# Blocks of 256 tokens: the activation's high half made by GpSimd, and one weight conversion moved from before the first block into it

## The chip, the cores and the metric

The kernel runs on one core of a Trainium2 chip. The metric is the device time of one execution in microseconds (us). A core has a matrix engine (TensorE, PE in the rows; its weight loads are PEld), a vector engine (VectorE, DVE), a scalar engine (ScalarE, ACT), a general engine (GpSimd, POOL) and a queue that only issues transfers here (SyncE, SP). Each engine takes its own instructions in a fixed order and waits on semaphores for the others.

## The reference, cut to what matters

Windowed causal attention feeds two MLPs in a row; everything is float32, the weights arrive as float64.

```python
# 4 batches, 8 heads, 576 positions, head size 64, window of 128 keys
scores = scale * q @ k.T ;  scores = where(mask, scores - slope*|i-j|, -1e9)
attn = exp(scores - max) ;  attn = attn / (attn.sum() + 1e-9)
x = attn @ v                                  # -> [2304 tokens, 512]
h = x @ w_in1                                 # [2304, 2048]
g = where(h >= 1, h, where(h <= -1, 0, (h + 1)**2 / 4))
x = g @ w_out1                                # [2304, 512]
h = x @ w_in2 ;  g = h * clip(h + 3, 0, 6) / 6
out = g @ w_out2
```

## The kernel before, in words

TensorE multiplies in a rounded float32 type, so every operand exists as two parts: a high half (the value rounded to that type) and a low half (the value less its high half). A product is the sum of three matmuls: low by high, high by low, high by high. The function `split_hi` (lines 150 to 156) makes a high half on a named engine: on ACT a copy (line 152), on "pool" a GpSimd multiplication by 1.0 (line 154). `split_lo` (lines 158 and 159) subtracts on a named engine.

The attention works in units of 64 to 256 query positions; unit 0 has 256 positions, two steps for each of the 8 heads, 16 steps in all. One `att.tick()` does one step's scores (stage a: matmuls at line 411, DVE bias and row minimum at 441, ACT exponential at 445) and the later stages of earlier steps (transposes at 469 and 470, copies at 152, product with the values at 506 or 554). For a pair of heads it then normalizes (518 to 520), transposes (531) and splits the result into x (152 and 159), one 128-row chunk of x for each pair. Units 0 to 3 go this way; later units use a longer one with more GpSimd work (389 to 403, 450, 488).

The first MLP takes tokens in blocks: three of 256 (0, 1 and 2), then four of 384. For every one of 16 chunks f of the hidden layer, `first` computes h (line 659, 12 matmuls), `activate` computes g (688 on DVE, 689 on ACT, 690 on DVE, high half at 691 on ACT, low half at 692 on GpSimd), and two chunks later `second` multiplies g with w_out (line 701, 12 matmuls). Blocks 0 and 1 are each done in two halves of 8 chunks, in the order 0A, 1A, 0Z, 1Z, since weights are still arriving; block 2 and the wide blocks take all 16 chunks.

The weights of chunk f (1 MB of float64) are loaded and converted in place. `conv_tick` (222 to 233) finishes chunk n-1 (`conv2`: DVE lines 205 and 212; `conv3`: ACT high half at 152, DVE low half at 159, the tile `wa`) and begins chunk n (`conv1`: ACT at 194 and 198, GpSimd at 197). A chunk f can be used once the tick numbered f+2 is through. Before the first block there are `n_pre` = 20 ticks of attention, t = 0 to 19 (lines 862 to 868); conversions are traced after t = 9, 14, 18 and 19. Inside half-blocks the function `spread` (870 to 883) calls conversion and attention ticks from a hook that runs twice per chunk, 16 times per half-block: after slot k, `ceil(conv * k / 16)` conversions are done.

SyncE issues its transfers in the order of the program. On the other engines a planner puts the instructions in order from modelled times: among those that it thinks ready, the one earliest in the program goes first, so a later one can fill a gap. Some instructions are tied behind others (`att.behind()`).

Of the kernel before, what the change touches and what calls it, by code (L numbers as in the profile page):

```python
# [29 lines left out]
HI = dict(v="act", th="act", xf="act", x="act", g="act", x2="act")  # L30
# [10 lines left out]
def tile_window_attention_two_mlps(  # L41
# [20 lines left out]
    KF = DFF // P  # L62
# [11 lines left out]
    N1, WIDE = 256, 384  # L74
# [75 lines left out]
    def split_hi(eng, hi, x):  # L150
        if eng == "act":
            nc.scalar.copy(hi, x)  # L152
        elif eng == "pool":
            nc.gpsimd.tensor_scalar(out=hi, in0=x, scalar1=1.0, scalar2=1.0, op0=ALU.mult, op1=ALU.mult)
        else:
            engines[eng].tensor_copy(hi, x)

    def split_lo(eng, lo, x, hi):
        engines[eng].tensor_tensor(out=lo, in0=x, in1=hi.bitcast(F32), op=ALU.subtract)  # L159
# [105 lines left out]
    unit_steps = [sum(1 for n, _ in steps if heads[n].unit == j) for j in range(len(units))]  # L265
# [406 lines left out]
    class Mlp1(Mlp):  # L672
# [11 lines left out]
        def activate(self, ps, n):  # L684


            r, g = self.tiles()
            nc.vector.tensor_scalar(out=r[:, :n], in0=ps[:, :n], scalar1=-1.0, scalar2=1.0, op0=ALU.max, op1=ALU.min)  # L688
            self.square = nc.scalar.activation(out=r[:, :n], in_=r[:, :n], func=AF.Square, bias=0.5, scale=0.5)  # L689
            self.larger = nc.vector.tensor_tensor(out=r[:, :n], in0=ps[:, :n], in1=r[:, :n], op=ALU.max)  # L690
            split_hi(HI["g"], g[:, 0, :n], r[:, :n])
            split_lo(LO[self.g_lo], g[:, 1, :n], r[:, :n], g[:, 0, :n])
            return g

# [139 lines left out]
    A, Z = range(KF // 2), range(KF // 2, KF)  # L834

    def run_block(mlp1, j, part, hook):
        for f in part:
            chunks.run(mlp1, j, f, part, j, lambda: hook(f, 0), lambda: hook(f, 1), att.behind)

    with ExitStack() as actx:  # L840
        mlp1 = Mlp1(W1, blocks1, rpool, gpool)
# [20 lines left out]
        n_pre = unit_steps[0] + LAG_D  # L862
        for t in range(n_pre):
            att.tick()
            if t % 2 == 0:
                W1.load()
            if t in (n_pre // 2 - 1, n_pre - 6) or t >= n_pre - 2:
                W1.conv_tick()

        def spread(part, ticks, conv):  # L870

            slots = 2 * len(part)
            att0, conv0 = att.t, W1.n_conv

            def hook(f, after):
                k = 2 * (f - part[0]) + after + 1
                W1.load()
                while W1.n_conv < conv0 + min(conv, -(-conv * k // slots)) and W1.conv_tick():
                    pass
                while att.t < att0 + min(ticks, -(-ticks * k // (slots - 2))):  # L880
                    att.tick()

            return hook
# [14 lines left out]

            return hook

        run_block(mlp1, 0, A, spread(A, unit_steps[1] + unit_steps[2], KF // 2 - 2))
        run_block(mlp1, 1, A, spread(A, 10, KF // 4))
        att.make_tables()
        run_block(mlp1, 0, Z, spread(Z, unit_steps[3] - 10, KF // 2))
# [259 lines left out]
    for m, blk, f, part, g in chunks.pend:  # L1164
        assert f == KF - 1
        t0, n = m.blocks[blk]
# [138 lines left out]
    for j, x in enumerate((xa, xb)):  # L1305
        block = Block(j, x)
        for i in range(KF // 2):
            def hook(n):
                if j == 0 and n == 0:
                    if 1 <= i <= 5:  # L1310
                        weight_sums(i + 2)
                    if i in (4, 6):
                        xb.load((i - 4) // 2)
                    if i in (6, 7):
                        xb.make(i - 6, lambda: ts.tile([P, N2], F32, tag="t", name="t"))
                spare((0.5, 0.8, 0, 0.8, 0, 0, 0.4)[n])
                load_operands()
# [30 lines left out]
```

## Time and profile before

| | |
|---|---|
| time, median of 3 runs (lowest to highest) | 946.75 us (946.28 to 947.42) |
| the profiled execution's own time | 946.02 us |
| span of its trace | 944.3 us |
| busy share of the span: PE, PEld, DVE, ACT, POOL | 98%, 93%, 70%, 57%, 32% |
| granted TensorE clock, mean | 1.000 |
| chain that ended last: PE, DVE, ACT, DMA, POOL | 89%, 5%, 2%, 2%, 1% |

Busy shares are means over stages that differ much, so the windows are read stage by stage. A matmul counts as busy from its issue to the end that the profile models, so a busy PE can still issue fewer matmuls than it could. The first matmuls of `first` run at about 23 us, the first instruction at line 688 starts at 36.17 us, half-block 0A lasts to about 75 us and the three blocks of 256 tokens to about 230 us. After 500 us there is no GpSimd work left.

### The profile page before, as it was taken

What the parts mean: (1) busy time and instruction counts of PE and PEld (TensorE: products, weight loads), DVE (VectorE), ACT (ScalarE), POOL (GpSimd) and SP (SyncE); (2) the same over time, 40 slices, a digit from 0 to 9 for tenths busy, and PEclk for the clock granted to TensorE, in tenths of its full rate; (3) what the DMA queues carried; (4) which work ended last, traced back from release to release, by engine and by line L of the source; (5) the groups of instructions that cost most, each with busy time, mean ns of one, the idle gap of its engine ahead of it and who ended that gap; (6) DMA issues with size and microseconds to landing.
All of it is one profiled execution on the core that took longest, in us unless ns stands there. A gap on an engine that the chain in (4) does not pass through costs nothing.

```text
span 944.3 us, 17237 instructions
## 1 busy us (share of the span) xinstructions
PE 928.5 (98%) x5683; PEld 875.5 (93%) x5683; DVE 659.4 (70%) x1750; ACT 535.6 (57%) x1349; POOL 306.8 (32%) x575
## 2 busy tenths in 40 slices
PE   8899999999999999999999999999999999999998
PEld 6799999999999999999999999999999888898987
DVE  6998975786677677767656899958557777644443
ACT  6998854676667566666635786535333334423233
POOL 3243845787668676777710000000000000000000
PEclk9999999999999999999999999999999999999999
DMA  8858322232222212322017771004264654543431
GB/s 256 240 178 264 111 89 88 68 86 67 73 64 72 79 46 62 89 75 62 1 55 270 266 237 55 1 23 167 81 210 170 232 174 146 169 124 114 123 112 67
DMA packets 95337, 114.90 MB, mean 122 GB/s; under 512 B 8848, under 2 KB 73616, under 8 KB 95248
## 3 DMA queue, kind: packets, MB, share of 16 engines
q1 hardware_dynamic: 95248, 113.80, 38.3%
q8 instruction: 45, 0.74, 0.3%
q14 instruction: 44, 0.36, 0.1%
HBM read 88.60 MB, written 25.17 MB: 120 GB/s over the span
## 4 chain that ended last, share of the span: by engine, by line
PE 89%; DVE 5%; ACT 2%; DMA 2%; issue 1%; POOL 1%; SPq 0%; ACTq 0%; DVEq 0%; POOLq 0%
PE h L659 26%; PE acc L760 21%; PE acc L701 18%; PE y L1249 7%; PE x L1249 5%; PE s L411 4%; PE r L554 3%; PE t L470 2%; PE r L506 2%; DMA rawa<-w_in 1%; DVE r L688 1%; DVE kl L391 1%; DVE r L690 1%; DVE x L159 1%; DMA kw<-kT 1%
## 5 line engine op out<-in xcount | busy, mean ns | idle before, releaser
L659 PE MATMUL h<-x,wa 128*128 128x384 f32 (+1 forms) x1344 | 231.0, 317 | 1.4 <-DVE r L690 0.9
L701 PE MATMUL acc<-g,wa 128*128 128x384 f32 (+1 forms) x1344 | 227.4, 315 | 0.4 <-POOL g L159 0.4
L760 PE MATMUL acc<-wb,g 128*128 128x512 f32 x861 | 222.2, 393 | 0.0
L659 PEld LDWEIGHTS h<-x,wa 128*128 128x128 f32 x1344 | 206.8, 189 | 4.3 <-DVE r L690 3.4
L701 PEld LDWEIGHTS acc<-g,wa 128*128 128x128 f32 x1344 | 206.3, 189 | 0.7 <-POOL g L159 0.6
L760 PEld LDWEIGHTS acc<-wb,g 128*128 128x128 f32 x861 | 159.4, 188 | 24.9
L152 ACT CAST g<-r 128x384 fp32r<-128x384 f32 (+1 forms) x208 | 101.6, 489 | 71.4 <-DVE r L1196 37.6
L159 POOL TENSOR_TENSOR g<-r,g 128x256 fp32r<-128x256 f32 (+1 forms) x96 | 92.5, 964 | 67.7 <-ACT g L152 54.8
L689 ACT ACTIVATE r<-r 128x384 f32<-128x384 f32 (+1 forms) x112 | 53.5, 479 | 81.3 <-DVE r L688 81.0
L159 DVE TENSOR_TENSOR g<-r,g 128x384 fp32r<-128x384 f32 x112 | 62.4, 557 | 41.9 <-ACT g L152 41.6
L688 DVE TENSOR_SCALAR r<-h 128x384 f32<-128x384 f32 (+1 forms) x112 | 55.4, 495 | 44.0 <-PE h L659 37.3
L488 POOL TENSOR_SCALAR_AFFINE_SELECT tt<-dist 128x256 fp32r<-128x256 f32 (+1 forms) x176 | 76.9, 458 | 13.9 <-DVE dist L483 13.8
L690 DVE TENSOR_TENSOR r<-h,r 128x384 f32<-128x384 f32 (+1 forms) x112 | 55.8, 499 | 30.3 <-ACT r L689 28.4
L659 PE MATMUL h<-x,wb 128*128 128x384 f32 x384 | 72.5, 336 | 0.0
L659 PEld LDWEIGHTS h<-x,wb 128*128 128x128 f32 x384 | 68.2, 188 | 2.6
L445 ACT ACTIVATE p<-p,sm 128x128 f32<-128x128 f32 (+2 forms) x134 | 57.3, 430 | 20.9 <-DVE sm L441 20.5
L1194 ACT ACTIVATE r<-u 128x384 f32<-128x384 f32 x32 | 16.9, 527 | 56.2 <-DVE u L1258 56.2
L554 PEld LDWEIGHTS r<-tt,vs 128*128 128x128 f32 x304 | 44.7, 189 | 3.2 <-issue 1.4
L393 POOL TENSOR_TENSOR qs<-qr,qs 128x256 fp32r<-128x256 f32 (+2 forms) x64 | 39.4, 616 | 24.9 <-ACT qs L390 13.3
L554 PE MATMUL r<-tt,vs 128*128 128x128 f32 (+3 forms) x304 | 44.3, 262 | 1.4 <-POOL tt L488 0.9
L470 PE MATMUL t<-ident,p 128*128 128x128 f32 x134 | 38.4, 288 | 0.5 <-ACT tt L152 0.5
L1249 PE MATMUL y<-wb,w 128*128 128x384 f32 x192 | 38.7, 336 | 0.0
(161 smaller groups left out, 1554.6 us busy)
## 6 DMA issues: line engine op xcount, KB each, us to landing
w<-wd SPq DMA_DIRECT2D x88, 256.0 KB, 2.7
rawa<-w_in SPq DMA_DIRECT2D x16, 512.0 KB, 5.3
rawa<-w_out SPq DMA_DIRECT2D x16, 512.0 KB, 5.4
rawb<-w_in SPq DMA_DIRECT2D x16, 512.0 KB, 3.8
rawb<-w_out SPq DMA_DIRECT2D x16, 512.0 KB, 4.7
wd<-sum SPq DMA_DIRECT2D x32, 256.0 KB, 2.1
wd<-wb SPq DMA_DIRECT2D x24, 256.0 KB, 2.8
out<-o SPq DMA_DIRECT2D x17, 256.0 KB, 2.3
```

What stands on the lines that cost most here:

```text
L152: nc.scalar.copy(hi, x)
L159: engines[eng].tensor_tensor(out=lo, in0=x, in1=hi.bitcast(F32), op=ALU.subtract)
L445: nc.scalar.activation(out=pt[:, :nk], in_=pt[:, :nk], func=AF.Exp, bias=sm[:, 0:1], scale=-1.0, accum_out=None if u.whole else sm[:, 1:2])
L470: nc.tensor.transpose(ps[:, 1, :], pt[:, P:] if u.whole and has_prev else pt[:, :P], ident)
L488: nc.gpsimd.affine_select(out=u.tt[:, :, s0 + s, :m], in_=both, compare_op=ALU.is_ge, fill=0.0, base=-1 + s, pattern=[[0, 2], [sign, m]], ...
L554: nc.tensor.matmul(u.r[:, qo:qo + nq], u.vs[:, j, c, :, :].rearrange("p a d -> p (a d)"), u.tt[:, part].rearrange("p s q -> p (s q)")[:, s ...
L659: nc.tensor.matmul(ps[:, :n], self.W.w_in(a, c, f), self.x_chunk(x, b, c, n), start=(k == 0), stop=(k == 3 * KC - 1))
L688: nc.vector.tensor_scalar(out=r[:, :n], in0=ps[:, :n], scalar1=-1.0, scalar2=1.0, op0=ALU.max, op1=ALU.min)
L690: self.larger = nc.vector.tensor_tensor(out=r[:, :n], in0=ps[:, :n], in1=r[:, :n], op=ALU.max)
L701: nc.tensor.matmul(acc[i][:, o * n:(o + 1) * n], self.W.w_out(a, f)[:, e * P:(e + 1) * P], g[:, b, :n], start=(first and k == 0 and o == 0 ...
L760: nc.tensor.matmul(acc[t][:, :DM], g[:, b, tg * P:(tg + 1) * P], self.W.w_out(a, f), start=(first and k == 0), stop=(last and k == 2))
L1249: nc.tensor.matmul(ps[:, :N2], w[:, a, c * P:(c + 1) * P], self.x.operand(k, c, b), start=(start and n == 0), stop=(n == 5), skip_group_ch ...
```

## The change

In blocks of 256 tokens the high half of g is made by GpSimd, with the instruction at line 154, in place of ACT's copy at line 152; there are 48 of these (3 blocks of 16 chunks). The wide blocks and the second MLP keep ACT. Before the first block there are three conversion ticks, after t = 9, 15 and 19, in place of four after t = 9, 14, 18 and 19. Half-block 0A has seven (after slots k = 1, 3, 5, 7, 10, 12, 14) in place of six (after k = 1, 3, 6, 9, 11, 14). Ten have been called at the end of 0A in both, and nothing else differs.

```diff
@@ Mlp1.activate
             self.larger = nc.vector.tensor_tensor(out=r[:, :n], in0=ps[:, :n], in1=r[:, :n], op=ALU.max)
-            split_hi(HI["g"], g[:, 0, :n], r[:, :n])
+            split_hi("pool" if n == N1 else HI["g"], g[:, 0, :n], r[:, :n])
             split_lo(LO[self.g_lo], g[:, 1, :n], r[:, :n], g[:, 0, :n])
@@ before the first block
             if t % 2 == 0:
                 W1.load()
-            if t in (n_pre // 2 - 1, n_pre - 6) or t >= n_pre - 2:
+            if t in (n_pre // 2 - 1, n_pre - 5, n_pre - 1):
                 W1.conv_tick()
@@ half-block 0A
-        run_block(mlp1, 0, A, spread(A, unit_steps[1] + unit_steps[2], KF // 2 - 2))
+        run_block(mlp1, 0, A, spread(A, unit_steps[1] + unit_steps[2], KF // 2 - 1))
```

## Rows read from the trace of the kernel before

**Rows 1.** The page, chain that ended last, shares by engine and line.
```profile
PE 89%; DVE 5%; ACT 2%; DMA 2%; issue 1%; POOL 1%; SPq 0%; ACTq 0%; DVEq 0%; POOLq 0%
```

**Rows 2.** Windows: start:end, length, busy us (instructions) by engine, PEclk, DMA, GB/s.
```profile
10.00:36.00 26.00, 22.04 (x148) 17.44 (x148) 20.66 (x59) 22.42 (x47) 5.89 (x6) 1.00 1.03 300
36.00:75.00 39.00, 37.50 (x299) 36.16 (x298) 36.28 (x96) 37.31 (x76) 16.85 (x22) 1.00 0.59 178
75.00:109.00 34.00, 33.52 (x280) 32.89 (x280) 30.66 (x74) 30.73 (x69) 18.81 (x21) 1.00 0.68 219
...
190.00:220.00 30.00, 29.55 (x244) 28.73 (x243) 24.58 (x98) 22.85 (x84) 26.79 (x57) 1.00 0.36 98
```

**Rows 3.** Timeline of DVE, 27 to 37 us: start, us, instruction [idle before <-releaser].
```profile
27.52 1.23 DVE L205 SCALAR_TENSOR_TENSOR ma<-ma,rawa 128x1024 uint32<-128x1024 uint32 x1 [0.21 <-POOL rawa L197]
28.67 0.42 DVE L441 CUSTOM_DVE_ANT_0 p<-s,dist 128x256 f32<-128x256 f32 x1
...
30.70 0.17 DVE L519 RECIPROCAL rec<-rec 128x4 f32<-128x4 f32 x1
30.79 1.19 DVE L212 CUSTOM_DVE_ANT_0 ma<-rawa,ma 128x2048 uint16<-128x2048 uint16 x1
31.90 0.42 DVE L520 TENSOR_TENSOR y<-r,rec 128x256 f32<-128x256 f32 x1
...
34.71 0.42 DVE L159 TENSOR_TENSOR x<-x,x 128x256 fp32r<-128x256 f32 x1
...
36.17 0.42 DVE L688 TENSOR_SCALAR r<-h 128x256 f32<-128x256 f32 x1
```

**Rows 4.** Timeline of ACT, 27 to 37 us.
```profile
31.09 1.20 ACT L194 ACTIVATE ma<-rawa 128x1024 f32<-128x1024 f32 x1
32.13 0.55 ACT L445 ACTIVATE p<-p,sm 128x256 f32<-128x256 f32 x1
```

**Rows 5.** Timeline of PE, 27 to 42 us.
```profile
29.15 0.70 PE L411 MATMUL s<-kw,qw 128*128 128x256 f32 x2 [1.01 <-DVE sm L441]
...
32.74 0.33 PE L469 MATMUL t<-ident,p 128*128 128x128 f32 x1 [0.55 <-ACT p L445]
...
33.01 0.38 PE L531 MATMUL x<-ident,y 128*128 128x128 f32 x2
...
35.18 0.51 PE L659 MATMUL h<-x,wa 128*128 128x256 f32 x2 [0.23 <-DVE x L159]
```

**Rows 6.** Groups by line and form, 0 to 330 us: count | busy us, mean ns | idle before.
```profile
L159 POOL TENSOR_TENSOR g<-r,g 128x256 fp32r<-128x256 f32 x48 | 42.0, 877 | 35.9 <-ACT g L152 27.9 <-issue 6.6 <-POOL p L450 0.7
...
L197 POOL TENSOR_SCALAR rawa<-rawa 128x1024 f32<-128x1024 f32 x16 | 23.6, 1475 | 39.5 <-ACT ma L194 22.2 <-DMA qw<-qT 8.8 <-DMA kw<-kT 4.6
...
L205 DVE SCALAR_TENSOR_TENSOR ma<-ma,rawa 128x1024 uint32<-128x1024 uint32 x16 | 21.3, 1334 | 1.5 <-POOL rawa L197 1.4
L159 DVE TENSOR_TENSOR wa<-ma,wa 128x1024 fp32r<-128x1024 f32 x16 | 21.0, 1312 | 0.4 <-ACT p L445 0.2
L212 DVE CUSTOM_DVE_ANT_0 ma<-rawa,ma 128x2048 uint16<-128x2048 uint16 x16 | 20.7, 1294 | 0.0
...
L152 ACT CAST g<-r 128x256 fp32r<-128x256 f32 x48 | 19.5, 405 | 9.7 <-DVE r L690 8.5 <-PE s L411 0.9
...
L198 ACT ACTIVATE rawa<-rawa 128x1024 int32<-128x1024 uint32 x16 | 18.6, 1163 | 0.0
L194 ACT ACTIVATE ma<-rawa 128x1024 f32<-128x1024 f32 x16 | 18.6, 1162 | 0.5 <-DMA rawa<-w_out 0.3 <-DVE wa L159 0.2
L152 ACT CAST wa<-ma 128x1024 fp32r<-128x1024 f32 x16 | 16.9, 1053 | 3.0 <-DVE ma L212 2.8
...
L142 POOL TENSOR_SCALAR dist<-rel 128x256 bf16<-128x256 f32 x8 | 3.2, 406 | 0.3
```

**Rows 7.** Timeline of all engines, 44 to 47 us: POOL and DVE.
```profile
45.08 0.75 POOL L159 TENSOR_TENSOR g<-r,g 128x256 fp32r<-128x256 f32 x1
45.15 1.76 DVE L205 SCALAR_TENSOR_TENSOR ma<-ma,rawa 128x1024 uint32<-128x1024 uint32 x1 [0.30 <-POOL rawa L197]
```

## The prediction

> **What bounds the kernel now.** I read the chain that ended last first, then the windows, then the timelines of the stretch in which the windows show free time on PE. The chain is PE for 89% of the span [rows 1], so only two things can move the end: time in which PE waits for work, and work that PE would have to do and does not (none here, the matmuls stay the same). The windows show where PE waits. From 36 to 109 us it is 96 to 99% busy, and just as busy from 190 to 220; in the 26 us from 10 to 36 it is 85% busy, with 148 matmuls, 5.7 per us, against 7.7 per us (299 in 39 us) in the stretch behind it [rows 2]. A busy PE counts overlapping matmuls, so the count says more than the share: at the later rate the 148 would take 19.3 us, so some 6.7 us are lost there, an estimate. In the same 26 us ACT is busy for 22.4 and DVE for 20.7 [rows 2]: the start is bound by those two engines, and PE waits in line for them. The stretch 36 to 75 (half-block 0A) is full on three engines at once, PE 37.5, ACT 37.3 and DVE 36.3 of 39 us, and the next one has 3.3 us free on each of DVE and ACT [rows 2]. So a change of who does what before 110 us can win little more than the 6.7 us, and can lose as soon as DVE is asked for more than it has in 0A.
>
> The gate at the start is x: the last of its four chunks is split by DVE at 34.71, the last matmuls of the first h follow at 35.18 with a wait on just that, and the first instruction at line 688 comes at 36.17 [rows 3, 5].
>
> **The conversion tick that leaves the start.** One tick costs ACT 1162 + 1163 + 1053 = 3.38 us, DVE 1334 + 1294 + 1312 = 3.94 us and GpSimd 1.48 us [rows 6]. The three ticks left come one tick of attention later or at the same place, so what stood in the way as the fourth tick (chunk 2 finished, chunk 3 begun) is what goes. The timelines show it between the instructions of the last pair of heads. On DVE, L205 at 27.52 holds up L441 at 28.67, for which PE's L411 waited 1.01 us; I count 0.5 of it, since the scores were computed only shortly before. Then L212 at 30.79 stands between the reciprocal L519 (done at 30.87) and L520 at 31.90: 1.03 us. Together 1.5 us [rows 3, 5]. On ACT, L194 at 31.09 holds the exponential L445 until 32.13, for which PE waited 0.55 us at L469, and the transposes of x at 33.01 are queued behind that on PE [rows 4, 5]: a parallel path of 1.04 us, which must go as well for the 1.5 us to count, and does. The second and third tick are traced later too, so fewer of their instructions come before x; I add 0.5 us for them. I take 2.0 us gained. Bounds: nothing, if the planner fills the free places with the next tick's instructions just as long; 3.9 us, all of DVE's work of one tick. Transfers don't move: SyncE keeps the program's order, and weights are issued from places that the change leaves alone. If SyncE's later issues wait on attention's buffers, those come free earlier, not later.
>
> **The tick that 0A gets.** DVE has 36.28 us of work there and gets 3.94 more, ACT 37.31 plus 3.38 less its eight copies of g (8 x 0.405 = 3.24), so ACT stays where it was [rows 2, 6]. DVE would need 40.2 us in 39: it is over by 1.2. Its last tick in 0A (chunk 8) is not needed until half-block 0Z, and 1A behind it has 3.3 us free on DVE, so part of the excess moves on without PE seeing it. I take a loss of 0.9 us, near the excess. Bounds: nothing lost (all of it moves to 1A), and 3.9 us (none of it is covered). The ticks in 0A also come up to two slots later than before (for chunk 4, slot 5 in place of 3), with first use after slot 8, so weights still come ahead; that cover ends if a slot's conversion takes longer than three slots of about 2.4 us (39 us by 16).
>
> **The high half on GpSimd.** ACT loses 48 x 0.405 = 19.4 us of work, GpSimd gets 48 of an instruction that the trace does not show in this form. The nearest row is the multiplication at L142 with the same shape, 406 ns [rows 6], so 48 x 0.406 = 19.5 us. What it is worth on the path is only what ACT's queue delays: of L689, which stands before the release of h's bank, and of the exponentials. In 0A and 1A ACT is relieved of 16 x 0.405 = 6.5 us while PE is already nearly full; I take 0.6 us gained, bounds nothing and 6.5. On GpSimd the queue behind the new instruction is the subtraction of the same g, and behind that the sign instruction at L197 and the later units' work. GpSimd idled 27.9 us in wait of ACT's g ahead of the subtraction [rows 6], and its wait now ends one engine earlier, so a rounding mostly fills time that was idle. The cover is thin from 190 to 220, where 26.79 of 30 us are busy [rows 2] and some 8 roundings add 3.2: GpSimd would be full.
>
> **What the two engines do to each other.** DVE's L205 at 45.15, started while GpSimd's subtraction of 45.08 ran, took 1.76 us against a mean of 1.33; and the subtraction takes 0.88 us on the mean against 0.75 there [rows 6, 7]. So a GpSimd instruction can cost a DVE instruction with two inputs in SBUF up to 0.43 us, and waits itself. A rounding is about half as long as a subtraction. I take 0.3 us lost in all, bounds nothing and 16 x 0.43 = 6.9 us (each rounding in 0A and 1A hits).
>
> The Trainium skill (SBUF — State Buffer, "SBUF: two separate sides") says that the two engines share one pair of ports as an exclusive lock: whichever of a GpSimd instruction and a VectorE instruction with two SBUF inputs starts first keeps it to its end, and the other stands still. The row at 45.15 agrees. By that rule a reading GpSimd instruction locks DVE out however simple it is, the new ones too; this speaks against the change and is the third rival below.
>
> **The sum.** -2.0 + 0.9 - 0.6 + 0.3 = -1.4 us. On the profiled execution's own 946.02 us (span 944.3 and 1.7 around it) this makes 944.6; that execution lies 0.7 under the median of the runs, 946.75, so for the median I forecast 945.3 us.
>
> **The rivals.** First, the gain stays whole: the start gives 2.0, the excess in 0A moves into the free 3.3 us of 1A (no 0.9), and relieving ACT gives 1.5 rather than 0.6, since ACT was the fuller of the two in both stretches up to 75 us. For it speaks that PE at 99% in 1A shows no wait that a late conversion could lengthen; against it that DVE is over its time in 0A. Sum -3.5: 943.2 us.
>
> Second, nothing arrives: the start is shorter by 2.0, 0A longer by all of the tick's uncovered part (about 2.0), since DVE's total before 110 us is unchanged and DVE is 93% busy there. For it speaks the sum of DVE's work; against it the 0.9 us that DVE's free time allows. 946.7 us.
>
> Third, the other side: GpSimd takes the lock from DVE. If half of the 16 roundings of 0A and 1A each hold up a conversion instruction, DVE loses 8 x 0.43 = 3.4 us in a stretch where it has none to give, and in 190 to 220 a full GpSimd with waits of 0.13 us for each of 8 roundings is late by 1.0 us with the later units' scores and values. With -2.0 and +0.9 that is +3.3: 950.0 us. It decides against the change from about 4 hits on (1.7 us, which with the other terms cancels the gain). For it speaks that DVE's instructions with two inputs fill over half of the time in 36 to 109 us (an estimate: the six ticks of 0A and the four of 1A, 10 x 3.94 us in 73); against it that a rounding is short, and that it runs right behind L690, when DVE itself is between things.
>
> **How the numbers follow.** The forecast's case has 0.48, the first rival 0.24, the second 0.11, the third 0.17. About 0.2%, 1.9 us, is what a measurement of this kernel can tell from no change. The forecast's case alone spans 943.9 to 946.5; a third of it (0.17) is faster than 944.86, the rest the same. With the first rival this gives faster 0.41; same 0.31 + 0.11 = 0.42; slower 0.17, the third rival. The range reaches from 942.4 (the first rival with the start at 2.8) to 949.2 (the third with 6 hits in place of 8).
>
> **What would show it.** In the profile after: the last split of x and the first L688 near 34 us in place of 34.71 and 36.17; if they stay, the first term is wrong. PE's count between 10 and 34 us at 5.7 per us or more. In 0A, DVE near 98% and the half-block some 1 us longer; if it is longer by 2 or more, the second rival holds. Roundings on GpSimd at about 0.41 us; if their mean is 0.6 or more and DVE's conversion instructions exceed 1.31 us on the mean, the third. Waits of PE on GpSimd between 190 and 220 us that were not there. The prediction is wrong if the three blocks' end, at about 230 us, moves by something other than what the start and 0A show, or if the wide blocks behind them change by more than 1 us.

## The result, and the profile after

| | before | after |
|---|---|---|
| time, median (lowest to highest), 4 runs each | 946.74 us (946.28 to 947.42) | 953.14 us (952.21 to 954.08) |
| span of the trace | 944.3 us | 950.8 us |
| granted TensorE clock, mean | 1.000 | 0.996 |

The change makes the kernel slower: after over before is 1.0068, interval 1.0055 to 1.0080, that is 6.4 us. Forecast were 945.3 us and a range up to 949.2.

The chain that ended last, shares by engine, answers to [rows 1]; PE's part is the same, and GpSimd's (POOL) has doubled:

```profile
PE 89%; DVE 4%; ACT 2%; POOL 2%; issue 2%; DMA 0%; ACTq 0%; POOLq 0%; DVEq 0%; SPq 0%
```

The windows of the kernel after (start:end, length, busy us and instructions of PE, PEld, DVE, ACT, POOL, then PEclk, DMA share, GB/s) answer to [rows 2]:

```profile
10.00:36.00 26.00, 21.98 (x148) 17.55 (x149) 20.20 (x59) 22.33 (x47) 5.92 (x6) 1.00 1.00 288
36.00:75.00 39.00, 37.12 (x280) 35.31 (x279) 35.05 (x89) 34.64 (x67) 21.43 (x27) 0.96 0.61 191
75.00:109.00 34.00, 32.75 (x275) 32.32 (x275) 31.33 (x75) 28.38 (x58) 20.73 (x26) 1.00 0.64 212
...
100.00:120.00 20.00, 16.67 (x137) 16.07 (x136) 17.24 (x33) 15.80 (x30) 18.33 (x18) 0.98 0.21 63
190.00:220.00 30.00, 29.60 (x246) 28.87 (x245) 25.36 (x99) 21.16 (x76) 28.32 (x61) 1.00 0.30 83
40.70:44.10 3.40, 3.40 (x15) 3.14 (x15) 2.31 (x7) 2.50 (x5) 2.01 (x4) 0.50 0.85 269
119.20:122.60 3.40, 2.97 (x14) 2.86 (x14) 2.88 (x9) 1.24 (x4) 3.08 (x5) 0.50 0.22 67
```

The stretch 100 to 120 was not among the rows read before; this is its window in the kernel before:

```profile
100.00:120.00 20.00, 19.57 (x165) 19.32 (x164) 19.89 (x39) 16.54 (x37) 17.65 (x14) 1.00 0.27 81
```

Three things are to be seen. In the start nothing moved: 148 PE instructions in the same 26 us. In 0A PE issues 280 in place of 299. DVE, which was to be near 98% busy there, is busy for 35.1 of 39 us, that is 90%, less than before. ACT, which was to stay level, falls from 37.3 to 34.6 us busy: its eight copies of g (8 x 0.405 = 3.2 us) have left, and no conversion work has come in their place (the counts are given with e12 and e13). And from 100 to 120, where the profile of before shows GpSimd at 17.65 of 20 us, PE issues 137 in place of 165. Of 190 to 220, where I had looked for a full GpSimd, nothing is lost (246 against 244). In two places of 3.4 us the granted clock is at 0.50, the 1.2 GHz level of its two (1.2 and 2.4 GHz); before had none ahead of its last microseconds.

The start. The timeline of DVE after (start us, duration us, instruction) answers to [rows 3]:

```profile
31.29 1.19 DVE L212 CUSTOM_DVE_ANT_0 ma<-rawa,ma 128x2048 uint16<-128x2048 uint16 x1
32.40 0.42 DVE L520 TENSOR_TENSOR y<-r,rec 128x256 f32<-128x256 f32 x1
...
33.99 1.23 DVE L205 SCALAR_TENSOR_TENSOR ma<-ma,rawa 128x1024 uint32<-128x1024 uint32 x1 [0.83 <-POOL rawa L197]
35.14 0.42 DVE L159 TENSOR_TENSOR x<-x,x 128x256 fp32r<-128x256 f32 x1
...
36.60 0.42 DVE L688 TENSOR_SCALAR r<-h 128x256 f32<-128x256 f32 x1
...
37.98 2.06 DVE L212 CUSTOM_DVE_ANT_0 ma<-rawa,ma 128x2048 uint16<-128x2048 uint16 x1
39.97 0.41 DVE L690 TENSOR_TENSOR r<-h,r 128x256 f32<-128x256 f32 x1
```

Up to the first L688 it is the same list, 0.4 to 0.5 us later: DVE's 79 instructions up to there are the same in the same order in both traces. The L212 that was to leave (chunk 2's, the third in both) still stands ahead of L520, though its tick is now traced in 0A. Behind it the order changes: L212 now comes ahead of L690 of the first chunk. It also took 2.06 us, for GpSimd had begun a sign instruction 0.12 us earlier (the first row of the next view but one), and PE stood still. PE's waits in the two places (the last bracket is idle time and releaser):

```profile
40.44 1.00 PE L659 MATMUL h<-x,wa 128*128 128x256 f32 x4 [1.46 <-DVE r L690]
...
118.93 0.38 PE L701 MATMUL acc<-g,wa 128*128 128x256 f32 x1 [1.85 <-POOL g L154]
119.74 2.71 PE L701 MATMUL acc<-g,wa 128*128 128x256 f32 x11 [0.43 <-POOL g L159]
```

The second place is GpSimd's queue, in its timeline after:

```profile
37.86 1.11 POOL L197 TENSOR_SCALAR rawa<-rawa 128x1024 f32<-128x1024 f32 x1 [3.90 <-ACT ma L194]
...
107.59 2.13 POOL L197 TENSOR_SCALAR rawa<-rawa 128x1024 f32<-128x1024 f32 x1
109.69 1.53 POOL L159 TENSOR_TENSOR vs<-vr,vs 128x192 fp32r<-128x192 f32 x1
111.19 0.41 POOL L154 TENSOR_SCALAR g<-r 128x256 fp32r<-128x256 f32 x1
111.67 1.59 POOL L159 TENSOR_TENSOR g<-r,g 128x256 fp32r<-128x256 f32 x1
113.22 1.72 POOL L393 TENSOR_TENSOR qs<-qr,qs 128x256 fp32r<-128x256 f32 x1
114.90 1.55 POOL L159 TENSOR_TENSOR vs<-vr,vs 128x192 fp32r<-128x192 f32 x1
116.43 2.09 POOL L197 TENSOR_SCALAR rawa<-rawa 128x1024 f32<-128x1024 f32 x1
118.47 0.41 POOL L154 TENSOR_SCALAR g<-r 128x256 fp32r<-128x256 f32 x1
118.96 0.73 POOL L159 TENSOR_TENSOR g<-r,g 128x256 fp32r<-128x256 f32 x1
```

The rounding at 118.47 is that of chunk 14. DVE had its input ready at 112.99 (L690 of that chunk, 112.58 and 0.41 long); it stood 5.5 us behind a query split, a value split and a sign instruction, with no gap between them. From 107.59 on nothing in this list waits: GpSimd is the bound here.

Groups of the kernel after, 0 to 330 us (mean ns is the number behind the busy time), answer to [rows 6]:

```profile
L197 POOL TENSOR_SCALAR rawa<-rawa 128x1024 f32<-128x1024 f32 x16 | 25.3, 1580 | 29.7 <-ACT ma L194 29.7
L154 POOL TENSOR_SCALAR g<-r 128x256 fp32r<-128x256 f32 x48 | 24.2, 505 | 33.7 <-DVE r L690 15.9 <-DVE rec L519 5.9 <-DVE x L159 3.0
L205 DVE SCALAR_TENSOR_TENSOR ma<-ma,rawa 128x1024 uint32<-128x1024 uint32 x16 | 21.4, 1339 | 2.0 <-POOL rawa L197 1.9
L212 DVE CUSTOM_DVE_ANT_0 ma<-rawa,ma 128x2048 uint16<-128x2048 uint16 x16 | 20.9, 1305 | 0.0
...
L159 DVE TENSOR_TENSOR wa<-ma,wa 128x1024 fp32r<-128x1024 f32 x16 | 22.1, 1381 | 0.3 <-ACT p L445 0.2
```

DVE's 48 conversion instructions take 64.4 us in place of 63.0 [rows 6]. GpSimd pays more: 505 ns on the mean for a rounding in place of the estimated 406, and 1580 for a sign instruction in place of 1475.

Where the time went, in every run's trace. Four marks divide it: DVE's first and last x split of unit 0, and PE's first matmul of `second` for chunks 7, 16 and 47 (0A holds chunks 0 to 7, 1A 8 to 15, 0Z 16 to 23, 1Z 24 to 31, block 2 32 to 47). The stretch from the last x split to chunk 7 is called 0A below, though it reaches some 10 us into 1A, since `second` comes two chunks after `first`. Microseconds between marks, worked out from the starts in the traces; the differences between runs of marks that nothing touches are about 0.2 us:

```
                     first to     last x to   chunk 7     chunk 16    clock at 0.50
                     last x       chunk 7     to 16       to 47       (start, length)
before               20.93        50.27       36.22       113.73      -
after                20.73        53.26       40.02       113.11      40.7, 3.4; 119.2, 3.4
e1  rounding alone   20.89        52.24       40.57       113.10      120.2, 3.4
e2  ticks alone      20.77        52.64       36.42       113.93      40.4, 3.4
e3                   20.84        53.58       35.96       113.11      40.4, 3.4
e4                   20.90        50.25       36.27       113.12      -
e6                   20.78        53.20       41.13       113.09      40.0, 3.4
e7                   20.89        52.63       35.90       113.89      -
e8                   18.62        57.71       37.47       114.01      39.1, 6.8
e9                   20.80        53.28       36.36       113.09      40.4, 3.4
e10                  19.18        54.31       35.88       114.67      -
e11                  20.89        51.27       37.82       113.19      -
e12                  20.81        50.25       36.21       113.92      -
e13                  20.88        52.64       36.43       113.94      40.9, 3.4
e14                  20.92        51.84       36.48       113.71      -
e15                  20.90        50.43       39.10       113.72      -
```

So after against before: the start -0.2, 0A +3.0, chunks 7 to 16 +3.8, chunks 16 to 47 -0.6, and -0.1 behind them. The two traces differ by 0.6 us more ahead of the first x split (14.40 in place of 13.77 us); that is no effect of the change, since this mark lies between 13.6 and 15.2 us in the sixteen traces and by 1.4 us apart in e15 and e4, which are alike up to there. The row of e8 is that of an execution with a fall of the clock, which four of its six do not have (see e8).

### The profile page after: what moved, and what is told of

Read it like the earlier page. It is cut to its first block, busy times and chain, and to the rows that moved or that the text cites. A ratio compares the mean times of both kernels' runs of the same rounds, so it can differ in the third digit from the quotient of the medians.

```text
span 950.8 us, 17240 instructions
## 1 busy us (share of the span) xinstructions
PE 931.9 (98%) x5683; PEld 878.4 (92%) x5683; DVE 661.5 (70%) x1750; ACT 521.6 (55%) x1301; POOL 331.1 (35%) x623
## 4 chain that ended last, share of the span: by engine, by line
PE 89%; DVE 4%; ACT 2%; POOL 2%; issue 2%; DMA 0%; ACTq 0%; POOLq 0%; DVEq 0%; SPq 0%
PE h L659 26%; PE acc L760 21%; PE acc L701 18%; PE y L1249 7%; PE x L1249 5%; PE s L411 4%; PE r L554 3%; PE t L470 2%; PE r L506 2%; POOL rawa L197 1%; DVE r L688 1%; DVE kl L391 1%; DVE r L690 1%; POOL g L159 0%; DVE x L159 0%
## 5 line engine op out<-in xcount | busy, mean ns | idle before, releaser
L152 ACT CAST g<-r 128x384 fp32r<-128x384 f32 x160 | 81.9, 512 | 62.2 <-DVE r L1196 37.6
L159 POOL TENSOR_TENSOR g<-r,g 128x256 fp32r<-128x256 f32 (+1 forms) x96 | 93.4, 973 | 35.1 <-ACT g L152 26.9
L688 DVE TENSOR_SCALAR r<-h 128x384 f32<-128x384 f32 (+1 forms) x112 | 55.5, 495 | 48.3 <-PE h L659 37.8
L690 DVE TENSOR_TENSOR r<-h,r 128x384 f32<-128x384 f32 (+1 forms) x112 | 55.8, 499 | 29.6 <-ACT r L689 27.7
```

## The experiments

Each time is a median beside the kernel before on the same chip (946.4 to 947.0 us).

**The two halves of the change: e1 and e2.** e1 is the kernel before with the rounding alone, e2 with the ticks alone.

```diff
# e1, on the kernel before
-            split_hi(HI["g"], g[:, 0, :n], r[:, :n])
+            split_hi("pool" if n == N1 else HI["g"], g[:, 0, :n], r[:, :n])
# e2, on the kernel before
-            if t in (n_pre // 2 - 1, n_pre - 6) or t >= n_pre - 2:
+            if t in (n_pre // 2 - 1, n_pre - 5, n_pre - 1):
...
-        run_block(mlp1, 0, A, spread(A, unit_steps[1] + unit_steps[2], KF // 2 - 2))
+        run_block(mlp1, 0, A, spread(A, unit_steps[1] + unit_steps[2], KF // 2 - 1))
```

> The kernel before with one half of the change: GpSimd rounds g in all 48 chunks of the blocks of 256, the conversion ticks stay as they were. Theory A (the changed kernel loses its 6.4 us in two places: some 3 us near 37 to 44 us, where DVE's order after the moved ticks leaves PE waiting for the first h bank, and some 4 us near 110 to 124 us, where GpSimd's queue is late with the rounding; in each place the granted clock falls after the wait and costs part of it): the second place stays, the first goes; 946.7 + 4.1 - 0.7 (the late blocks ran shorter by that) = about 950 us. Rival B (the moved ticks make both waits): no slower than before, 946 to 947 us. Rival C (roundings hold up DVE's conversions everywhere, spread over 36 to 125 us): about 952 us, with no single wait of PE over 1 us.

e1: 952.45 us, ratio 1.0061 (1.0047 to 1.0075), 5.6 over before. The time is rival C's, the picture is not: PE's wait on GpSimd at the second place is there (1.86 us). Theory A missed the 2.0 us that 0A loses in e1 too.

> The kernel before with the other half: one conversion tick less ahead of the first block and one more in half-block 0A, g rounded by ACT throughout. Theory A: the first place stays if it comes from the order of DVE after the moved ticks, the second goes: about 947 + 2.5 = 949 us, with the granted clock down once near 41 us; the first instruction at line 688 stays near 36.2 us, since the planner filled the start with as many conversion instructions as before. Rival B: the whole loss, about 953 us. Rival C: no loss, about 947 us.

e2: 949.35 us, ratio 1.0027 (1.0018 to 1.0037), 2.6 over before. It is what theory A expected. Both halves lose, the rounding most. 5.6 and 2.6 make 8.2, and the change costs 6.4; the three intervals don't exclude a plain sum, but the traces do for 0A, where +2.0 and +2.4 make +3.0 together.

**Taking back the rounding where GpSimd is full: e3.** The kernel after, with ACT rounding in 1A and 0Z.

```diff
-            split_hi("pool" if n == N1 else HI["g"], g[:, 0, :n], r[:, :n])
+            split_hi("pool" if n == N1 and not 8 <= i < 24 else HI["g"], g[:, 0, :n], r[:, :n])
```

> The changed kernel, but ACT rounds g in half-blocks 1A and 0Z (16 of the 48 chunks), GpSimd in the other 32. Theory A: the wait near 117 us and the fall of the clock behind it go, the first place stays: 953.1 - 4.1 = about 949 us. Rival B (ticks): still about 953 us. Rival C (spread over all roundings): a third of the loss goes, about 951 us.

949.73 us, ratio 1.0032 (1.0019 to 1.0045): 3.4 of the 6.4 us come back, the stage from chunk 7 to 16 is at 35.96, and the wait at 118.9 and the clock's fall behind it are gone.

**The rounding in block 2 alone: e4** (the kernel before, `n == N1 and i >= 32`).

```diff
-            split_hi(HI["g"], g[:, 0, :n], r[:, :n])
+            split_hi("pool" if n == N1 and i >= 32 else HI["g"], g[:, 0, :n], r[:, :n])
```

> The kernel before with GpSimd rounding g only in block 2 (16 chunks, about 169 to 235 us), where the changed kernel ran some 0.7 us shorter than the kernel before in spite of a GpSimd that is busy for over 28 of 30 us from 190 to 220. Theory A: both places are as in the kernel before, 946.7 - 0.7 = about 946.0 us. Rival C: a third of the loss, about 949 us. The third rival of the prediction (GpSimd too full from 190 to 220 us): 1 us slower than before, 947.7 us.

946.40 us, ratio 0.9994 (0.9985 to 1.0003): no loss though GpSimd is busy for 29.1 of the 30 us from 190 to 220, and in the trace the stage is 0.6 us shorter:

```profile
190.00:220.00 30.00, 29.59 (x247) 28.87 (x246) 25.31 (x98) 21.68 (x80) 29.11 (x65) 1.00 0.35 98
```

A full GpSimd alone is no loss.

**The rounding in 0A alone and in 1A and 0Z alone: e14 and e15** (as e4, with `i < 8` and with `8 <= i < 24`).

```diff
-            split_hi(HI["g"], g[:, 0, :n], r[:, :n])
+            split_hi("pool" if n == N1 and i < 8 else HI["g"], g[:, 0, :n], r[:, :n])       # e14
+            split_hi("pool" if n == N1 and 8 <= i < 24 else HI["g"], g[:, 0, :n], r[:, :n]) # e15
```

> The kernel before with GpSimd's rounding in half-block 0A alone (chunks 0 to 7); the conversion ticks stay where they were. Theory A (the rounding's loss is made in 1A and 0Z, where GpSimd also converts and prepares the later units): within 0.5 us of before, 946.8 us. Rival B (GpSimd's lock on DVE, or its later low half, costs in the half-block that is full on three engines): 948.3 us or more. Rival C (ACT's relief is worth something there, as my term of -0.6 had it): 946.0 us or less.

> The kernel before with GpSimd's rounding in half-blocks 1A and 0Z alone (chunks 8 to 23). Theory A (all of the loss of the rounding is made here): 951.5 to 952.5 us, as with the rounding everywhere (952.45). Rival B (it is shared with 0A): 950 us. If GpSimd's queue costs as much with the conversion ticks of before as with those of the change, where ACT's rounding in these chunks gave back 3.4 us: 950.2 us.

e14: 948.41 us, ratio 1.0019 (1.0010 to 1.0028), +1.9, its rival B. e15: 949.76 us, ratio 1.0035 (1.0021 to 1.0048), +3.3, as the last line of its expectation has it. With e4 the parts make 1.9 + 3.3 - 0.4 = 4.8 of e1's 5.6; the rest is within the intervals. So the rounding loses in 0A too, without any fall of the clock, in a stretch where GpSimd is busy for 18.05 of 39 us (e14's window 36 to 75). The groups of L154 show how the rounding itself fares, in e14 (0A), e15 (1A, 0Z) and e4 (block 2), one fence each:

```profile
L154 POOL TENSOR_SCALAR g<-r 128x256 fp32r<-128x256 f32 x8 | 4.3, 533 | 3.1 <-DVE r L691 3.1
```

```profile
L154 POOL TENSOR_SCALAR g<-r 128x256 fp32r<-128x256 f32 x16 | 9.6, 598 | 13.4 <-DVE r L691 9.8 <-DVE sm L448 1.8 <-DVE rec L518 1.5
```

```profile
L154 POOL TENSOR_SCALAR g<-r 128x256 fp32r<-128x256 f32 x16 | 6.5, 403 | 2.2 <-DVE r L691 1.8 <-DVE dist L483 0.2
```

403 ns without DVE's conversion beside it, 533 and 598 on the mean with it (the last section shows what these means are made of). In 0A PE waits no longer in e14 than before (1.82 us in all against 1.77); it is busy for longer, with 391 matmuls between the two marks in place of 386. What makes the 1.6 us there is open.

In 1A e15 loses its 2.9 us in another way than the change. Its waits of PE on GpSimd's g are 0.71 us in all; the longest is 1.00 us on DVE's split of x. That split stood behind an L205 which waited 0.82 us for GpSimd's sign instruction, and then took 2.13 us beside the next one:

```profile
104.19 2.13 DVE L205 SCALAR_TENSOR_TENSOR ma<-ma,rawa 128x1024 uint32<-128x1024 uint32 x1 [0.82 <-POOL rawa L197]
```

```profile
108.11 0.33 PE L469 MATMUL t<-ident,p 128*128 128x128 f32 x1 [1.00 <-DVE x L159]
```

**What fills GpSimd's queue: e9.** The kernel after, with the sign instruction of chunks 12 to 15 on ACT (the weights of these chunks lose their sign, the rest of the work stays).

```diff
-                nc.gpsimd.tensor_scalar(out=sign, in0=sign, scalar1=0.0, scalar2=1.0, op0=ALU.mult, op1=ALU.mult)
+                if f >= 12:
+                    nc.scalar.activation(out=sign, in_=sign, func=AF.Copy, scale=0.0)
+                else:
+                    nc.gpsimd.tensor_scalar(out=sign, in0=sign, scalar1=0.0, scalar2=1.0, op0=ALU.mult, op1=ALU.mult)
```

> The changed kernel with the sign instruction (L197) of the last four chunks' conversions on ACT in place of GpSimd; the roundings stay on GpSimd. Theory A as refined by the earlier runs (roundings and signs together are more than GpSimd can do from 100 to 120 us, and the rounding of the 15th chunk stands in the queue for over 5 us behind L690): the wait at 119 us and its fall of the clock go, 953.1 - 3.5 = about 949.6 us. Rival (a rounding is late because of the lock with DVE alone, whatever else stands in GpSimd's queue): the wait stays, about 953 us.

949.59 us, ratio 1.0026 (1.0017 to 1.0036), as its theory A had it. The roundings stay on GpSimd, four sign instructions go, and the same 3.5 us come back. GpSimd's timeline:

```profile
112.88 0.41 POOL L154 TENSOR_SCALAR g<-r 128x256 fp32r<-128x256 f32 x1 [1.58 <-DVE r L693]
113.37 1.59 POOL L159 TENSOR_TENSOR g<-r,g 128x256 fp32r<-128x256 f32 x1
114.92 1.73 POOL L396 TENSOR_TENSOR qs<-qr,qs 128x256 fp32r<-128x256 f32 x1
```

and PE's, where the product that had waited 1.85 us starts at once:

```profile
117.05 0.39 PE L414 MATMUL s<-kw_kl,qw 128*128 128x128 f32 x2
117.19 1.68 PE L704 MATMUL acc<-g,wa 128*128 128x256 f32 x12
```

GpSimd now idles for 1.58 us ahead of chunk 14's rounding, in wait of its input (DVE's L693 here). That the change's loss in 1A needs both the roundings and the sign instructions on GpSimd is shown by this run and e3 together. But four sign instructions less can also hold up DVE four times less, as e15's rows show, so how much is the queue and how much that isn't separated.

**The ticks, divided: e12 and e13.** e12 only moves the second tick by one step and keeps four ticks before the block; e13 only takes one tick out of the start into 0A.

```diff
# e12, on the kernel before
-            if t in (n_pre // 2 - 1, n_pre - 6) or t >= n_pre - 2:
+            if t in (n_pre // 2 - 1, n_pre - 5) or t >= n_pre - 2:
# e13, on the kernel before
-            if t in (n_pre // 2 - 1, n_pre - 6) or t >= n_pre - 2:
+            if t in (n_pre // 2 - 1, n_pre - 6, n_pre - 1):
...
-        run_block(mlp1, 0, A, spread(A, unit_steps[1] + unit_steps[2], KF // 2 - 2))
+        run_block(mlp1, 0, A, spread(A, unit_steps[1] + unit_steps[2], KF // 2 - 1))
```

> The kernel before with one conversion tick moved by one step: four ticks before the first block, after t = 9, 15, 18 and 19 in place of 9, 14, 18 and 19, and six in 0A as before. No work is moved into 0A. Theory A (the conversion edit lost time since a tick more has to be done in 0A): no difference, 946.6 us. Theory B (the order of before fits together up to chunk 16, and any tick moved at the start makes the planner fill the places behind it in another order, with many small waits of PE): 948.5 us or more though the amount of work in every stage is unchanged.

> The other half of the conversion edit: three ticks before the first block, after t = 9, 14 and 19 (the one after t = 18 is gone, the second stays), and seven in 0A as in the change. Theory A (the tick more in 0A costs its 2 us, the second tick's place nothing): 949 us, and the last x split stays 20.9 us behind the first. Theory B (the order decides, not the amount): another time than e2's 949.35 by 1 us or more, to either side. Neither theory expects it under 946 us.

e12: 946.88 us, ratio 0.9997 (0.9988 to 1.0006). e13: 949.55 us, ratio 1.0029 (1.0019 to 1.0038), with 0A at 52.64 as in e2. The times are those of theory A: the second tick's place is worth nothing, and the whole loss comes with the tick that is traced in 0A. Its reason, that 0A has more work, is not what the traces show. DVE's L212 between the last x split and chunk 7's `second`, in the kernel before and in e2 (window, its length, DVE's busy us and count, PEclk, DMA share, GB/s):

```profile
34.71:84.98 50.27, 8.47 (x7) 1.00 0.63 196
```

```profile
35.00:87.64 52.64, 9.45 (x7) 0.97 0.63 199
```

The other conversion instructions that start there are as many, too: DVE does 7 + 7 + 8 of L205, L212 and the low half in before, e2, e12, e13 and after alike, and ahead of the last x split four, three and two. The planner left the moved tick's instructions where they ran before, and in e12 it leaves every conversion of DVE within 0.1 us of its place beside the last x split, so e12 moved nothing. In e2 and e13 it is the order in 0A that changes: chunk 3's low half starts 11 us behind the last x split in place of 4.2. How this order makes 2.4 us is open: PE idles 0.4 us more, and is busy for longer, with 5 matmuls more between the marks and the 3.4 us at 0.50.

**Is it the stand-still at 40 us and the clock? e7.** e2 with the DVE instructions of the fifth tick tied behind the first chunk's L690.

```diff
-                while W1.n_conv < conv0 + min(conv, -(-conv * k // slots)) and W1.conv_tick():
-                    pass
+                while W1.n_conv < conv0 + min(conv, -(-conv * k // slots)):
+                    with ExitStack() as behind:
+                        if W1.n_conv == 4:
+                            behind.enter_context(tc.issue_after(first_larger[0].ins))
+                        if not W1.conv_tick():
+                            break
```

> The moved ticks alone (ACT rounds g), with VectorE's instructions of the first tick after the first chunk's activation (chunk 3 finished) tied behind that activation's last instruction, so that L212 can't stand ahead of it. Theory A: the wait of PE for the first h bank (1.46 us) and the fall of the clock behind it (1.7 us) go: 949.35 - 2.5 = about 946.9 us. Rival (the moved tick itself costs, DVE having too much to do in 0A): the loss comes back later in 0A, about 949 us.

948.87 us, ratio 1.0018 (1.0010 to 1.0027). The wait of 1.46 us and the fall of the clock are gone, and 0A is as long as in e2 (52.63 and 52.64). So the stand-still, which looks like the cause in the trace, is only the form that the loss takes: where it is prevented, 0A loses the same time in another way: PE idles 1.2 us more than before in small waits (the longest 0.84 us), and the rest is lost in a busy PE. Only 0.5 us was won, and the two intervals overlap.

**Is a start without the tick worth anything? e8 and e10.** e8 is e2 with ticks 4 and 5 tied behind the last x split (their DVE instructions); e10 is the kernel before with the one L212 that my first term had counted, placed behind L520.

```diff
# e8, on e2
+                    with ExitStack() as behind:
+                        if W1.n_conv in (3, 4):
+                            behind.enter_context(tc.issue_after(att.last_x.ins))
...
# e10, on the kernel before
+            with ExitStack() as behind:
+                if f == 2 and self.sign_pool:
+                    behind.enter_context(tc.issue_after(att.scaled.ins))
+                nc.vector.tensor_tensor(out=m.bitcast(I32), in0=m.bitcast(I32), in1=raw.bitcast(I32)[..., 0], op=ALU.add)
```

> The moved ticks alone, with VectorE's instructions of the two ticks after the first three (chunks 2 and 3 finished) tied behind the last split of x of unit 0, so that none of them can fill a gap at the start. If the planner's filling is why the start got no shorter, the time from the first split of x to the last (20.9 us before, 20.7 changed) falls by 1.5 us or more, the prediction's first term; if the start is bound by something else (attention's own chain, the transfers), it stays within 0.3 us. The total time depends on where the instructions then land: 945 to 949 us.

> The kernel before with one edit: DVE's addition L212 of chunk 2 (30.79 in the trace of before, between the reciprocal L519 and the scaling L520 of the last pair of heads) has its place behind that scaling. My term counted this addition at 1.03 us on the path to x. Theory A (the term was right in its mechanism, wrong only because the planner put another tick's instruction into the same place): the last x split comes about 1.0 us earlier after the first one than the 20.9 us of before, and the kernel takes about 945.8 us. Theory B (the DVE work of the conversion is conserved: what leaves the way of x stands in the way of the first chunks): the last x split comes up to 1.0 us earlier, and the kernel takes 946.8 us as before. Rival C: as with the ticks held behind x, PE then waits for a late wa and its clock falls: 948.5 us or more.

e8: 950.16 us, ratio 1.0046 (1.0030 to 1.0061). Two of its six executions, the one in the table among them, took 953.92 and 953.99 us at a mean granted clock of 0.995; the other four took 949.60 to 950.34 at 1.000. e10: 949.95 us, ratio 1.0035 (1.0022 to 1.0047). In both x comes earlier, by 2.3 and by 1.75 us, and in both the kernel is slower than before by over 3 us, e8 beyond the 945 to 949 us that it was expected to take. e10's timeline of DVE shows the edit at work:

```profile
31.56 0.42 DVE L523 TENSOR_TENSOR y<-r,rec 128x256 f32<-128x256 f32 x1
31.90 1.22 DVE L215 CUSTOM_DVE_ANT_0 ma<-rawa,ma 128x2048 uint16<-128x2048 uint16 x1
...
33.62 0.42 DVE L159 TENSOR_TENSOR x<-x,x 128x256 fp32r<-128x256 f32 x1 [0.16 <-ACT x L152]
```

and its window of 0A what it costs, with the clock at 1.00 and 278 PE instructions against 299:

```profile
36.00:75.00 39.00, 36.46 (x278) 33.93 (x279) 36.70 (x85) 35.26 (x71) 15.12 (x20) 1.00 0.53 166
```

This falls beside all three of e10's cases: A's earlier x is there, but not its gain; C's loss is there, but not its fall of the clock. Why 0A answers to one instruction's place with 4.0 us is not settled: PE idles 1.1 us more there in small waits (the largest 0.77 us), and is busy for longer with 397 matmuls between the marks in place of 386.

**The clock by itself: e6.** The kernel after with 16 idle matmuls on PE, meant to lie in the wait at 118.9.

```diff
+    def fill(mlp, n, ins):
+        with tc.issue_after(ins):
+            for _ in range(n):
+                nc.tensor.matmul(mlp.ps[:, 2 * P:], zeros[:, :P], zeros, start=False, stop=False, skip_group_check=True)
...
+                if mlp is mlp1 and blk == 1 and f == 6:
+                    fill(mlp, 16, mlp.last_h.ins)
```

> The changed kernel with 16 idle matmuls added on PE (into columns of a bank that nothing reads), placed ahead of the second product of the 15th chunk, where PE stood still for 1.85 us and the granted clock then was 0.50 for 3.4 us. Theory A (the clock falls because PE stood still): the wait shrinks to a few tenths of a us and the granted clock stays at 1.00 near 119 us; since at half speed 3.4 us hold 1.7 us of work, about 953.1 - 1.7 = 951.4 us, the idle matmuls lying in time that was lost anyway. Rival (the fall comes for another reason, such as the load of all engines at that place): the clock falls all the same, 953 to 955 us.

953.50 us, ratio 1.0080 (1.0065 to 1.0094). It failed as a test: the idle matmuls got their place behind the wait, not in it. But it showed something else. PE waited as long as in the kernel after, and the clock did not fall:

```profile
119.17 0.39 PE L702 MATMUL acc<-g,wa 128*128 128x256 f32 x1 [1.84 <-POOL g L154]
119.97 1.58 PE L702 MATMUL acc<-g,wa 128*128 128x256 f32 x11 [0.42 <-POOL g L159]
...
122.35 1.92 PE L783 MATMUL h<-zeros 128*128 128x256 bf16 x16
```

The stage from chunk 7 to 16 is 41.13 us with 1.92 us of idle matmuls in it, that is 39.2 without, against 40.02 in the kernel after: an estimate of 0.8 us for the fall itself. It is one of two that the runs allow. The other is e8's, within one kernel: its executions at 0.995 took 4.0 us longer than those at 1.000, and the trace of one has 6.8 us at 0.50, which at half speed would make 3.4. The waits that went with the fall are in that figure. (e6 itself has one execution of 956.54 us at a mean clock of 0.996, beside three of 953.42 to 953.52 at 0.998; it left no trace.)

**Both places out at once: e11.** The kernel after with e3's selection and e7's tie.

```diff
-            split_hi("pool" if n == N1 else HI["g"], g[:, 0, :n], r[:, :n])
+            split_hi("pool" if n == N1 and not 8 <= i < 24 else HI["g"], g[:, 0, :n], r[:, :n])
...
+                        if W1.n_conv == 4:
+                            behind.enter_context(tc.issue_after(first_larger[0].ins))
```

> The changed kernel with both places of loss taken out at once: the DVE instructions of conversion tick 5 stand behind chunk 0's L690 (as in e7), and ACT rounds g in chunks 8 to 23 (as in e3). GpSimd still rounds in 0A and in block 2. Theory A (the two places are all there is, apart from the tick's own late work): the trace has no fall of the clock near 40 and none near 119, and the time is that of e7, 948.9 us. Theory B (the rounding costs something in 0A and block 2 as well, by the lock): 950.5 us or more. Theory C (the second place's gain needs the first place's loss): 951 to 952 us.

949.25 us, ratio 1.0027 (1.0018 to 1.0036). The time is nearest to theory A's (2.8 us over the kernel before beside it, where e7 had 1.9), its picture is not: 0A is only 1.0 us over before, and a wait on GpSimd's low half has come back in the other place, again with the clock at 1.00:

```profile
117.26 1.58 PE L702 MATMUL acc<-g,wa 128*128 128x256 f32 x11 [1.98 <-POOL g L159]
```

No experiment points to a version that beats the kernel before: e4, the best, can't be told from it.

## Why the prediction was wrong

By its own steps, with the size that each was given and the one that the runs give:

| step | predicted, bounds | measured | where |
|---|---|---|---|
| the tick leaves the start | -2.0 (0 to -3.9) | -0.2, no more than runs differ | after; -0.05 in e13 |
| 0A gets a tick | +0.9 (0 to 3.9) | +2.4, with no more work there | 0A in e2, e13, e7 |
| high half: ACT's queue relieved | -0.6 (0 to -6.5) | +1.6 in 0A, +2.9 from 7 to 16, -0.6 behind | e14, e15, e4 |
| lock of DVE and GpSimd | +0.3 (0 to 6.9) | +1.4 of DVE's busy time | groups after |

**The start.** The working named its lower bound, "nothing, if the planner fills the free places with the next tick's instructions just as long", and that is what came. I had the sentence on the planner (the earliest in the program among those ready goes first) and took 2.0 all the same, because I took the place where a tick is traced for the time at which it runs. Traced in 0A, the tick's instructions still ran in the old places ahead of the last x split: DVE's list up to the first L688 did not change by one instruction. By the prediction's own sign (the last split at 35.14 and L688 at 36.60, not near 34) the term is wrong. The mechanism behind the term was right: where the place is kept free, x comes 1.75 to 2.3 us earlier (e10, e8). The gain from it is not: 0A gave back more.

**0A.** The step failed in its mechanism as well as its size. It added 3.94 us of DVE's work to 0A, and no such work came: DVE does 22 conversion instructions there before and after, and in the window from 36 to 75 us it is busy for 35.1 us in place of the 40.2 of the sum. The ticks alone lengthen 0A by 2.4 us all the same, and the stage behind it by 0.2 (e2, e13). That is near the "about 2.0" of the second rival, but by luck: its reason was the amount of DVE's work, and its other half, the shorter start, did not come either. What changed is the order in which the planner placed the same work; e10, where the place of one instruction makes the kernel 3.5 us slower with all work unchanged, shows that order alone can do this. How it does is open.

**The high half.** This is the step that failed by most, and by its sign: -0.6 was forecast, and the roundings alone cost 5.6 us (e1). I wrote that GpSimd's wait "now ends one engine earlier, so a rounding mostly fills time that was idle". That compares sums. In order, the new instruction put the high half, which `second` needs, behind whatever GpSimd holds at that moment, and in 1A that is up to 2.1 us of sign instruction and the splits of the later units (e3, e9). For the 1.6 us in 0A, where GpSimd was far from full, the runs show the loss and not its cause (e14). The cover was called thin from 190 to 220, where it did no harm; from 100 to 120, where GpSimd was 88% busy before (17.65 of 20) and the weights were still being converted, I hadn't looked. What ACT's relief is worth can be seen only in block 2: -0.6 us, by chance the number I had set for 0A and 1A.

**The lock.** Of the third rival the sign was right and the place wrong. It took the lock from DVE; DVE lost 1.4 us in all, most of it in the low half of the weights (1381 ns in place of 1312). GpSimd lost: 48 roundings at 505 in place of 406 ns are 4.8 us, 16 sign instructions at 1580 in place of 1475 are 1.7. Five roundings make up 4.6 of the 4.8; three of these lie in 0A (at 49.98, 57.26 and 64.47 us), two at 95.27 and 121.98. Its 1.0 us from 190 to 220 did not come (e4).

**The range** ended at 949.2, since I had no case in which both edits lose and the start gives nothing. Each edit by itself already lies beyond it (949.35 and 952.45).

## What to carry to other kernels

Before work goes to an engine with idle time, read that engine's queue in the stretch where the result is needed, one instruction after the other: what stands ahead of the new one, and for how long, is its price, not its own duration. Where a planner places the work, moving a piece of it in the program need not move it in time: count the instructions in the stretch afterwards before giving a gain or a loss to their amount. And a stand-still or a fall of the clock that a trace shows isn't a cause until a run without it has got its time back: here one such run got 0.5 us of 2.6.

## What the runs showed of the hardware

**A GpSimd rounding beside DVE's conversion has two lengths.** In the kernel after 43 of the 48 roundings took 0.40 to 0.63 us, and all but one of these at most 0.43. The other five took 1.24 to 1.49 us, and each of the five began together with an L205 or a low half of the weights on DVE, or up to 0.25 us behind its start. So the means (505 ns here, 533 in e14, 598 in e15) are mixtures: one long one of 8 in e14, three of 16 in e15, none in e4. Where the rounding began first, it kept its 0.4 us, and in three such cases the L205 beside it took 1.38 to 1.50 us in place of the usual 1.22. One pair of each kind, DVE's rows first, then GpSimd's:

```profile
49.90 1.19 DVE L205 SCALAR_TENSOR_TENSOR ma<-ma,rawa 128x1024 uint32<-128x1024 uint32 x1
...
86.52 1.38 DVE L205 SCALAR_TENSOR_TENSOR ma<-ma,rawa 128x1024 uint32<-128x1024 uint32 x1
```

```profile
49.98 1.37 POOL L154 TENSOR_SCALAR g<-r 128x256 fp32r<-128x256 f32 x1 [2.86 <-DVE rec L519]
...
86.42 0.40 POOL L154 TENSOR_SCALAR g<-r 128x256 fp32r<-128x256 f32 x1 [3.04 <-DVE x L159]
```

And DVE's L212 took 2.06 us behind a sign instruction that reads one tensor only. By the Trainium skill (SBUF — State Buffer, "SBUF: two separate sides") whichever starts first, a GpSimd instruction or a VectorE instruction with two SBUF inputs, keeps the shared ports to its end, and the other stands still. The traces agree, with the two lengths above.

**Waits of the same length, with the clock's fall and without.** After 1.85 us of waiting the clock stood at 0.50 for 3.4 us in the kernel after; after 1.84 us in e6 and 1.98 us in e11 it stayed at 1.00. What decides between them is open. Nor do the runs give one price for a fall: e6 against the kernel after makes it some 0.8 us for 3.4 us at 0.50, less than the 1.7 of half speed, and e8's executions with and without a fall make it 4.0 us for 6.8 us, more than the 3.4 of half speed.
